# The unread matmuls of the first stage in plain fp32 and in smaller lots, with new order tables

## The chip, the cores and the metric

The kernel runs on one core of a Trainium2 chip. The metric is the device time of one execution in microseconds, the median over several runs. A separate execution was taken by the hardware profiler; all spans, waits and durations below come from it. TensorE (PE) multiplies, VectorE (DVE) and ScalarE (ACT) do the elementwise work, GpSimd (POOL) clears and copies a few tiles at the start, and SyncE (SP) issues the DMAs.

## The reference

```
kv  = einsum('bhsd,bhse->bhde', k, v)             # 8 batches, 8 heads, 576 rows, 64 columns
out = einsum('bhsd,bhde->bhse', q, kv)
att = out / sqrt(mean(out*out, -1) + 1e-6) * g_norm
x   = att with the heads joined                   # 8 x 576 x 512
u   = x + ((x^T @ U) @ V)^T                       # rank 32, over the sequence
res = u + relu(u @ w_ch1) @ w_ch2                 # 512 -> 2048 -> 512
```

## The kernel before, in words

Two heads make a pair, four pairs make a batch, and the 4608 rows of the output are worked off in nine blocks of 512 columns (index `j`). Blocks 0 to 2 go through a plain two-layer product in 16 steps `f`: `ffn1` (12 matmuls of 512 columns, from the rows' high and low parts `uth`, `utl` and the weight tile `ws`f into the PSUM tile `h`), then `relu` on ACT and DVE into `hhl`, then `ffn2` (12 matmuls into four tiles `y`). Blocks 3 to 8 go two at a time through a product with seven forms of the weights instead of eight. Every fp32 value that a matmul reads at speed is split into a high and a low fp32r part, which costs ACT and DVE work.

The weights come as 64-bit numbers. For each `f` a DMA brings `raw`f; ACT copies its top bits (`dec0<-raw`), DVE shifts the rest into place (`dec1<-raw`), ACT makes the high part (`ws<-dec`) and DVE the low part.

Everything ahead of the first full `ffn1` is the first stage (`first_stage`). There each pair p of batch 0 passes through: `kv` (ten matmuls of 64 columns into `pp`), `kvc` (ACT copies into `kvb`), `out` (four matmuls into `y` and one into `pp`), `sq` (ACT squares into `x`), `red` (DVE sums), `root` (ACT), `rms` (DVE, four short instructions), `mul` (DVE, writes the normed `x`), `turn` (four matmuls against the unit matrix, back into `y`), `t` (five matmuls against `U`), `t4` (casts into `st`), `mix` (adds the rank-32 part to `y`), `uh` and `ul` (high and low part of the block's rows), and a `tail` of 64 columns. Tiles of pair 0 to 3 are `y_174` to `y_177`; the normed rows are `x_90` for pair 0 and `x123` for the others. The weights of `f` = 0 (`w1raw`, `w2raw`) are decoded here too, and step `f` = 0 of `ffn1` into `pp_172` is part of this stage. The first instruction of the main loop on PE is `ffn1` of `f` = 1, the first row `h<-uth,ws`.

No scheduler orders the instructions. Every step has a number in a table: `PAIR0`, `ONCE` and `RAWS` for the first stage and the raw loads, `DECODE`, `DUOS`, `PREP`, `CPAT`, `REST`, `FORMSAT` and `FOLLOW` for what is threaded between the blocks' matmuls. `at(place, step)` files a step and `do(limit)` calls all filed steps below a limit in ascending order. An engine's program is the order of these calls. Each engine runs its own in order and waits on semaphores for the others.

Some matmuls write to a PSUM tile that nothing reads (`spare`, called `h_109` in the rows of the order). The first eight (`WARM`) multiply the cleared tile `kvb[0]` in fp32, ahead of everything else. The others are the steps `x0` to `x7` of `ONCE`: each calls `fill()`, eight matmuls of the cleared tile `t4s[1]` with itself in fp32r. A matmul of plain fp32 appears in the trace as two passes, one of fp32r as one.

From batch 1 on, two pairs are worked off together by `run_step` (matmuls into `ph` and `pt`, after which the next `kv_sb` tile is read), then `sq`, `red`, `rms`, `mul` on `x_90`, then `t_both` (`pt<-x,u`). `kv_sb` has one buffer, so its next load waits until `run_step` has read the last.

Of the kernel before, what the change touches and what calls it, by code (L numbers as in the profile page):

```python
# [10 lines left out]
F32 = mybir.dt.float32  # L11
# [26 lines left out]
REST = {0: 3.7, 1: 51.3, 2: 83.9, 4: 112.05, 6: 169.0}  # L38
RESTLOAD = {1: 39.6, 2: 72.15, 4: 102.5, 6: 162.85}
FORMSAT = {3: ((89.5, 89.96, 90.05, 90.15, 92.95, 93.05, 93.25, 96.15, 96.95, 97.45, 98.95), (91.45, 91.61, 93.35, 94.3, 94.45, 96.3, 96.6, 97.8, 97.85, 98.85, 100.6)), 5: ((144.15, 146.21, 148.3, 148.9, 150.4, 151.4, 151.6, 153.25, 153.85, 154.45, 155.35), (146.55, 146.91, 148.75, 149, 149.45, 150.4, 151.45, 152.15, 152.8, 154.2, 154.55)), 7: ((195.4, 198.66, 199.8, 202.4, 204.35, 205.25, 206.4, 207.55, 208.35, 208.45, 212.25), (200.55, 201.51, 205.9, 205.95, 206.65, 206.75, 207.25, 207.6, 208.45, 209.3, 211.05))}  # L40
FINISH = {0: (37.15, 36.85, 35.7, 37.2), 1: (65.76, 68.34, 67.85, 68.25), 2: (101.5, 101.6, 100.75, 101.6)}
DECODE = ((-16.9, -13.1, -6.25, -3.1), (-3.4, -2.25, 0.35, 1.76), (0.55, 1.97, 2.98, 3.33), (3.34, 3.54, 4.29, 5.84), (5.45, 5.9, 6.45, 6.6), (6.11, 7.96, 8.21, 8.66), (8.47, 8.72, 8.77, 9.72), (10.08, 10.68, 11.63, 12.53), (11.1, 12.64, 13.04, 13.49), (13.05, 13.65, 14.1, 14.4), (14.36, 15.76, 16.21, 17.76), (17.77, 17.92, 20.57, 21.02), (20.13, 21.83, 22.63, 23.03), (22.79, 23.54, 24.14, 24.42), (24.15, 25.45, 27.54, 29.1))
FOLLOWERS = ('relu11_0', 'B11_0', 'relu12_0', 'B21_0', 'less11_0', 't2_0', 'less12_0', 'less21_0', 'relu11_1', 'B11_1', 'relu12_1', 'B21_1', 'less11_1', 't2_1', 'less12_1', 'less21_1', 'T2_0', 'T2_1', 'T1_0', 'T1_1', 'T3_0', 'T3_1', 'B22_0', 'B22_1', 'T4_0', 'T4_1')
FOLLOW = {
# [6 lines left out]
FIRSTKV = 2.95  # L51
GROUPS = ('kvl', 'ql', 'run', 'sq', 'kvc', 'red', 'root', 'rms', 'mula', 'mulb', 't', 'ts', 'turna', 'outa', 'ina', 'turnb', 'outb', 'inb', 't4a', 'mixa', 'adda', 'ga', 't4b', 'mixb', 'addb', 'gb')
DUOS = {
# [14 lines left out]
FORMS = ["A11", "A12", "S2", "S1", "S3", "S4", "A22"]  # L68
WITH = ["B11", "B21", "T2", "T1", "T3", "B22", "T4"]
PREP = ((31.2, 31.35, 33.05, 33.4), (34.4, 36.4, 38.1, 39.45), (36.75, 41.55, 43, 43.7), (42.3, 44.65, 45.3, 46.05), (45.4, 45.65, 46.7, 47.45), (49.95, 50.7, 52.4, 54.45), (52, 53.45, 55.3, 55.55), (55.95, 56.4, 57.25, 57.9), (59.7, 59.8, 61.25, 61.85), (60.1, 62.35, 62.95, 64.15), (63.35, 63.95, 65.35, 65.55), (67.31, 71.35, 71.75, 71.95), (70.95, 72.1, 74.7, 77.05), (75.85, 76.35, 78.15, 80.3), (81.25, 81.95, 84.2, 87.1), (81.95, 87.2, 88.95, 90.65))  # L70
CPAT = [35.8, 31.0, 10.74, 21.85, 14.9, 22.55, 41.95, 23.29, 27.65, 18.45, 27.55, 40.7, 34.95, 31.45, 25.3, 55.7]
WARM = 8
PAIR0 = ((-38.3, -37.9, -35.35, -34.35, -30.7, -30.6, -29.2, -29.1, -22.35, -28.55, -27.15, -23.3, -21.5, -18.45, -13.7, -13.9, -6.45), (-34.6, -33.2, -31.6, -28.95, -28.75, -28.1, -27.3, -25.65, -22.4, -25.15, -23.65, -20.8, -14.4, -12.4, -11.3, -13.99, -7.83), (-29.05, -27.35, -25.5, -24.45, -24.2, -23.45, -22.8, -21.75, -20.75, -21.1, -19.2, -18, -16.6, -11.6, -10.65, 0.56, 0.8), (-28.25, -26.95, -23.4, -23.15, -21.5, -20.85, -19.55, -19.35, -15.15, -18.65, -17.25, -14, -13.5, -11.2, -3.55, -3.47, -2.1))
ONCE = {'uvt': -35.4, 'uvb': -34.1, 'uvu': -31.3, 'vsh': -28.8, 'vsl': -23.5, 'v4': -22.8, 'w1t': -26.5, 'w1b': -25.6, 'w1h': -24.25, 'w1l': -19.25, 'w2t': -23.2, 'w2b': -17.4, 'w2h': -14.4, 'w2l': -4.15, 'f0': -11.85, 'f1': -8.7, 'f2': -7.1, 'x0': -10.85, 'x1': -36.45, 'x2': -31.85, 'x3': -32.4, 'x4': -23.95, 'x5': -40.25, 'x6': -30.55, 'x7': -16.09}
RAWS = (-24.25, -21.45, -11.75, -33.85, 6.9, 3.95, -19.93, 12.43, -17.56, 13.25, 13.81, 10.92)
LOADS = ['kv0', 'q0', 'uv', 'kv1', 'q1', 'kv2', 'q2', 'kv3', 'q3', 'w10', 'w20', 'w11', 'w21', 'w12', 'w22', 'w13', 'w23', 'kv4']
NBLK = B * S // BLK


@with_exitstack  # L80
def build(ctx: ExitStack, tc: tile.TileContext, kv0_in, kv_in, q_in, uv_in, w_in, out):
# [624 lines left out]
    def first_stage():  # L706
# [53 lines left out]
        def fill():  # L760
            for _ in range(8):
                mm(spare[:, 0:P], lhsT=t4s[1], rhs=t4s[1], start=True, stop=True)

        for k in range(8):
            once[f"x{k}"] = fill
# [297 lines left out]
```

## Time and profile before

| | us |
|---|---|
| median of three runs | 827.26 |
| the three runs | 828.61, 827.26, 824.36 |
| the profiled execution | 826.27 |
| its span, first to last instruction | 824.5 |
| PE busy in the span | 818.3 |

The profile's page gives each engine's busy time, its busy share in 40 slices and the granted TensorE clock, the DMA queues, and the chain of work that ended last. The trace behind it answers for stretches: instructions in order of time, the waits and what ended them, and busy times in windows. A matmul's busy time includes its way through the array, so its rate is read from the distance of starts, or from the chain, which counts each stretch once. The column of the granted clock shows 1.00 from the first microsecond on; where the level changes inside the first 15 us is seen only in the distances of the matmuls.

### The profile page before, as it was taken

The page shows a single profiled execution, that of the slowest core. Times are in us where ns is not written, and L with a number is a line of the kernel's source. Part 1 is how long each engine was busy: PE and PEld are TensorE (multiplying, and loading weights), DVE is VectorE, ACT ScalarE, POOL GpSimd, SP SyncE. Part 2 cuts the span into 40 slices and gives each one's busy share as a digit, 9 for nine tenths or more (in the row PEclk, how much of TensorE's full clock was granted, in tenths as well). Part 3 has the DMA queues.
Part 4 walks back from the last instruction along what each step waited for, and adds up shares of the span by engine and source line. Part 5 has one row for each costly group of instructions (what it writes and reads, how often), then busy time and mean ns, then how long its engine had stood idle before and what let it go on. Part 6 is the DMA issues. An engine that isn't in the chain of part 4 may idle for free.

```text
span 824.5 us, 13843 instructions
## 1 busy us (share of the span) xinstructions
PE 818.3 (99%) x5308; PEld 675.2 (82%) x5308; DVE 565.8 (69%) x840; ACT 355.3 (43%) x603; POOL 7.7 (1%) x38
## 2 busy tenths in 40 slices
PE   9999999999999999999999999999999999999998
PEld 9888788788887888887888888888788888888886
DVE  2867566777877566678855798579537974872485
ACT  3855543234323434444525554453255544331541
POOL 3000000000000000000000000000000000000000
PEclk9999999999999999999999999999999999999999
DMA  9956874957767645598789699786676786666665
GB/s 352 410 200 240 306 271 141 329 194 238 246 238 248 206 143 175 148 358 284 258 252 282 183 301 305 228 285 200 199 209 207 220 278 193 180 201 197 196 203 174
DMA packets 109841, 195.34 MB, mean 237 GB/s; under 512 B 10832, under 2 KB 45904, under 8 KB 107984
## 3 DMA queue, kind: packets, MB, share of 16 engines
q1 hardware_dynamic: 109632, 194.33, 72.5%
q8 instruction: 42, 0.69, 0.3%
q14 instruction: 23, 0.19, 0.1%
q10 hardware_dynamic: 144, 0.13, 0.0%
HBM read 145.14 MB, written 49.28 MB: 236 GB/s over the span
## 4 chain that ended last, share of the span: by engine, by line
PE 91%; DMA 4%; DVE 3%; ACT 1%; issue 0%; SPq 0%; DVEq 0%; ACTq 0%
PE y L132 68%; PE h L132 14%; PE pt L132 3%; PE ph L132 3%; DMA ut<-xt 2%; PE pp L132 2%; DMA raw<-w_in 2%; DVE dec L122 1%; DMA w1s<-dec 1%; DVE st L122 1%; SPq L122 0%; ACT dec L122 0%; DVE hhl L122 0%; DVE ut L122 0%; DVE ss L122 0%
## 5 line engine op out<-in xcount | busy, mean ns | idle before, releaser
L132 PE MATMUL y<-entry,ring 128*128 128x512 f32 x576 | 135.3, 390 | 0.0
L132 PE MATMUL y<-hhl,ws 128*128 128x512 f32 x540 | 131.3, 392 | 0.0
L132 PEld LDWEIGHTS y<-entry,ring 128*128 128x128 f32 x576 | 107.7, 188 | 22.7 <-issue 0.2
L132 PE MATMUL h<-uth,ws 128*128 128x512 f32 x360 | 119.1, 392 | 0.1
L132 PEld LDWEIGHTS y<-hhl,ws 128*128 128x128 f32 x540 | 100.3, 188 | 21.7 <-issue 0.6
L122 ACT ACTIVATE hhl<-h 128x512 fp32r<-128x512 f32 (+1 forms) x53 | 34.5, 651 | 121.6 <-PE h L132 109.1
L132 PE MATMUL y<-uB,ringw 128*128 128x512 f32 x354 | 84.7, 390 | 0.0
L122 DVE TENSOR_TENSOR h<-y,h 128x512 f32<-128x512 f32 x71 | 48.5, 688 | 51.9 <-PE y L132 43.3
L132 PE MATMUL y<-uT,ring 128*128 128x512 f32 x348 | 83.2, 391 | 0.0
L132 PEld LDWEIGHTS h<-uth,ws 128*128 128x128 f32 x360 | 67.5, 188 | 15.2 <-DVE hhl L122 1.1
L122 DVE TENSOR_TENSOR entry<-h,entry 128x1024 fp32r<-128x1024 f32 x48 | 58.0, 1219 | 31.6 <-ACT entry L122 29.5
L132 PEld LDWEIGHTS y<-uB,ringw 128*128 128x128 f32 x354 | 66.3, 188 | 13.7
L132 PEld LDWEIGHTS y<-uT,ring 128*128 128x128 f32 x348 | 64.9, 188 | 14.1 <-issue 0.4
L122 DVE SCALAR_TENSOR_TENSOR hhl<-h,hhl 128x512 fp32r<-128x512 f32 (+1 forms) x53 | 39.7, 749 | 49.6 <-ACT hhl L122 49.6
L132 PE MATMUL h<-utl,ws 128*128 128x512 f32 x180 | 70.1, 389 | 0.0
L122 ACT COPY h<-y 128x512 f32<-128x512 f32 x70 | 40.6, 587 | 63.4 <-PE y L132 63.3
L122 ACT CAST entry<-h 128x1024 fp32r<-128x1024 f32 x48 | 49.9, 1051 | 40.3 <-PE y L132 23.4
L132 PE MATMUL y<-entry,ringw 128*128 128x512 f32 x216 | 55.3, 391 | 0.0
L132 PE MATMUL y<-hhl,ringw 128*128 128x512 f32 x216 | 54.9, 389 | 0.0
L132 PE MATMUL y<-uT,ringw 128*128 128x512 f32 x210 | 50.6, 390 | 0.0
L132 PEld LDWEIGHTS y<-hhl,ringw 128*128 128x128 f32 x216 | 40.5, 188 | 8.5
L132 PEld LDWEIGHTS y<-entry,ringw 128*128 128x128 f32 x216 | 40.1, 188 | 8.6 <-issue 0.4
(169 smaller groups left out, 1054.3 us busy)
## 6 DMA issues: line engine op xcount, KB each, us to landing
ring<-wd SPq DMA_DIRECT2D x69, 256.0 KB, 3.4
kv_sb<-kv_in SPq DMA_DIRECT2D x14, 1216.0 KB, 7.7
ringw<-wd SPq DMA_DIRECT2D x66, 256.0 KB, 3.4
raw<-w_in SPq DMA_DIRECT2D x30, 511.8 KB, 11.3
ring<-w1s SPq DMA_DIRECT2D x48, 256.0 KB, 3.8
ringw<-w1s SPq DMA_DIRECT2D x48, 256.0 KB, 3.6
ring<-w2s SPq DMA_DIRECT2D x48, 256.0 KB, 4.0
ringw<-w2s SPq DMA_DIRECT2D x48, 256.0 KB, 4.1
```

What stands on the lines that cost most here:

```text
L122: ins = getattr(self.eng, name)(*args, **kw)
L132: ins = nc.tensor.matmul(*args, **kw)
```

## The change: fill matmuls and all order tables

The step `fill` now makes two matmuls in place of eight, and reads the cleared tile as fp32 (two passes each) and not as fp32r. There are fourteen such steps, `x0` to `x13`, and not eight. `WARM` is as it was. All order tables have new numbers. Every other instruction on every engine is there as often as before.

```diff
@@ first_stage @@
+        blank = t4s[1].bitcast(F32)
+
         def fill():
-            for _ in range(8):
-                mm(spare[:, 0:P], lhsT=t4s[1], rhs=t4s[1], start=True, stop=True)
+            for _ in range(2):
+                mm(spare[:, 0:P], lhsT=blank, rhs=blank, start=True, stop=True)
 
-        for k in range(8):
+        for k in range(14):
             once[f"x{k}"] = fill
@@ one of the tables; the others are renumbered in the same way @@
-RAWS = (-24.25, -21.45, -11.75, -33.85, 6.9, 3.95, -19.93, 12.43, -17.56, 13.25, 13.81, 10.92)
+RAWS = (-26.05, -34.85, -12.05, -24.35, 0.8, 10.4, -15.08, 11.83, -22.16, 14.9, 14.61, 16.57)
```

On PE, at the start of the program. `h_109` is the unread tile, `kvq0` and `kvq1` the data of pairs 0 and 1, `kvb` the copied products. Before:

```order
L132 MATMUL h_109<-kvb_102 128x128 x8
L132 MATMUL h_109<-t4_1_98 128x128 x8
L132 MATMUL pp_178<-kvq0_144 64x64 x10
L132 MATMUL h_109<-t4_1_98 128x128 x8
L132 MATMUL y_174<-kvb_102,kvq0_144 128x128 x4
L132 MATMUL pp_178<-kvb_102,kvq0_144 128x128
L132 MATMUL pp_179<-kvq1_148 64x64 x10
L132 MATMUL h_109<-t4_1_98 128x128 x16
L132 MATMUL y_175<-kvb_102,kvq1_148 128x128 x4
```

and after the change:

```order
L132 MATMUL h_109<-kvb_102 128x128 x8
L132 MATMUL h_109<-t4_1_98 128x128 x4
L132 MATMUL pp_178<-kvq0_144 64x64 x10
L132 MATMUL h_109<-t4_1_98 128x128 x2
L132 MATMUL y_174<-kvb_102,kvq0_144 128x128 x4
L132 MATMUL pp_178<-kvb_102,kvq0_144 128x128
L132 MATMUL h_109<-t4_1_98 128x128 x2
L132 MATMUL pp_179<-kvq1_148 64x64 x10
L132 MATMUL h_109<-t4_1_98 128x128 x2
L132 MATMUL y_175<-kvb_102,kvq1_148 128x128 x4
L132 MATMUL pp_179<-kvb_102,kvq1_148 128x128
L132 MATMUL h_109<-t4_1_98 128x128 x4
```

The work on the pairs stands in the same order; the unread lots between them have shrunk.

On PE, from the normed rows of pairs 1 and 2 on, up to the first part of `ffn1` (`pp_172`), after the change. `wf` is the unit matrix or `U`, `st0` to `st2` the `t4` tiles of pairs 1 to 3:

```order
L132 MATMUL h_109<-t4_1_98 128x128 x2
L132 MATMUL pp_178<-x123_119,wf_103 96x128 x5
L132 MATMUL y_176<-wf_103,x123_119 128x128 x4
L132 MATMUL y_175<-wf_103,x123_119 128x128 x4
L132 MATMUL h_109<-t4_1_98 128x128 x2
L132 MATMUL y_175<-v4_99,st0_134 128x4x64 x2
L132 MATMUL pp_179<-x123_119,wf_103 96x128 x5
L132 MATMUL h_109<-t4_1_98 128x128 x2
L132 MATMUL y_176<-v4_99,st1_135 128x4x64 x2
L132 MATMUL y_177<-wf_103,x123_119 128x128 x4
L132 MATMUL y_177<-v4_99,st2_136 128x4x64 x2
L132 MATMUL h_109<-t4_1_98 128x128 x2
```

Before, there is one unread lot of eight in the stretch that corresponds; now there are four lots of two up to here.

On DVE, around the first `run_step` of batch 1, before (`h_704` is the first-layer product of `f` = 5, `ss_774` the sums of the squares):

```order
L122 SCALAR_TENSOR_TENSOR hhl_717<-h_704,hhl_717 128x512
L122 TENSOR_REDUCE ss_774<-x_90 128x18
L122 SCALAR_TENSOR_TENSOR dec1_784<-raw8_648,dec0_104 128x1024
L122 RECIPROCAL r0_775<-ta_776 128x18
```

and after the change (`h_628` is that of `f` = 4, `h_727` that of `f` = 5):

```order
L122 SCALAR_TENSOR_TENSOR hhl_641<-h_628,hhl_641 128x512
L122 TENSOR_TENSOR ws6_701<-dec1_626,ws6_701 128x4x256
L122 SCALAR_TENSOR_TENSOR dec1_708<-raw7_321,dec0_104 128x1024
L122 TENSOR_TENSOR ws7_710<-dec1_708,ws7_710 128x4x256
L122 TENSOR_REDUCE ss_698<-x_90 128x18
L122 SCALAR_TENSOR_TENSOR hhl_740<-h_727,hhl_740 128x512
L122 SCALAR_TENSOR_TENSOR dec1_743<-raw8_471,dec0_104 128x1024
L122 RECIPROCAL r0_699<-ta_700 128x18
```

The `run_step` follows step 4 now and followed step 5 before, and DVE does three decode instructions and a `relu` between its release and the sums' use. On SP, the loads from `raw6` on, after the change (before, `raw9` stood directly behind `raw6` and ahead of both `ut32` loads):

```order
L122 DMA raw6_420<-w_in 128x2047 x2
L122 DMA raw8_471<-w_in 128x2047 x2
L122 DMA ut32_0_91<-q_in 128x576
L122 DMA ut32_1_92<-q_in 128x576
L122 DMA kv_sb_572<-kv_in 128x2432
L122 DMA kv_sb_746<-kv_in 128x2432
L122 DMA ut32_2_93<-q_in 128x576
L122 DMA ut32_3_94<-q_in 128x576
L122 DMA raw9_754<-w_in 128x2047 x2
```

`raw9` has moved behind two `kv_sb` loads, the second of which waits for `run_step`.

## Rows read from the trace of the kernel before

**Rows 1.** The page: engines, busy us, share of the span, instructions.

```profile
PE 818.3 (99%) x5308; PEld 675.2 (82%) x5308; DVE 565.8 (69%) x840; ACT 355.3 (43%) x603; POOL 7.7 (1%) x38
```

**Rows 2.** Waits of PE: us in total, times, longest.

```profile
PE h L132 <- DVE eps L122: 1.1, 1, 1.1
PE ph L132 <- DVE ut L122: 1.0, 2, 0.8
PE ph L132 <- ACT kvb L122: 0.4, 1, 0.4
```

**Rows 3.** PE in order of time: start, busy us, engine, what [idle before].

```profile
1.05 3.78 PE L132 MATMUL h<-kvb 128*128 128x128 f32 x16 [1.05 <-DVE eps L122]
4.49 1.95 PE L132 MATMUL h<-t 128*128 128x128 f32 x8
6.37 1.34 PE L132 MATMUL pp<-kvq 128*64 128x64 f32 x20
...
38.60 0.48 PE L132 MATMUL h<-uth,ws 128*128 128x512 f32 x1
```

**Rows 4.** The chain of waits, first 60 us: start, net us, what.

```profile
9.60 1.81 PE y L132 x8
...
13.11 2.34 PE h L132 x16
...
23.47 0.94 PE y L132 x8
...
27.01 1.09 PE pp L132 x10
...
31.16 1.19 PE y L132 x10
32.35 1.18 PE pp L132 x6
...
45.84 2.72 PE h L132 x12
```

**Rows 5.** ACT and DVE in the first stage, in order of time.

```profile
11.95 0.26 ACT L122 ACTIVATE x<-pp 64x128 f32<-64x128 f32 x1
12.31 0.82 DVE L122 TENSOR_REDUCE wf<-x 128x10 f32<-128x640 f32 x1 [2.71 <-ACT x L122]
...
14.01 0.22 DVE L122 RECIPROCAL wf<-wf 128x10 f32<-128x10 f32 x1 [0.89 <-ACT wf L122]
...
15.55 0.27 DVE L122 TENSOR_TENSOR x<-pp,wf 64x128 f32<-64x128 f32 x1
...
19.48 0.43 ACT L122 COPY kvb<-pp 64x64 f32<-64x64 f32 x2 [1.05 <-PE pp L132]
...
20.95 0.77 ACT L122 CAST dec<-w1raw 128x512 f16<-128x512 bf16 x1
21.74 0.60 ACT L122 ACTIVATE x<-y 128x512 f32<-128x512 f32 x1
...
25.23 1.28 ACT L122 CAST v<-uvs 32x144 fp32r<-32x144 f32 x4
```

**Rows 6.** Loads of the pairs' data (`kvq`), from issue to landing.

```profile
DMA to landing us min/median/max: 3.9/6.5/8.6
```

**Rows 7.** Behind the first `run_step` of batch 1, in order of time.

```profile
67.44 3.02 PE L132 MATMUL y<-hhl,ws 128*128 128x512 f32 x12
67.92 1.35 DVE L122 TENSOR_REDUCE ss<-x 128x18 f32<-128x1152 f32 x1 [1.39 <-ACT x L122]
...
74.45 0.68 DVE L122 TENSOR_TENSOR x<-ph,r 128x512 f32<-128x512 f32 x1
...
78.55 0.85 PE L132 MATMUL pt<-x,u 128*32 128x128 f32 x20
...
84.28 1.36 ACT L122 CAST dec<-raw 128x1024 f16<-128x1024 bf16 x1 [1.47 <-DMA raw<-w_in]
```

**Rows 8.** The chain of waits in the same stretch.

```profile
71.37 12.83 DMA raw<-w_in
```

More of the change, by code (lines that the diff above doesn't have):

```diff
@@ L37 @@
 NEARLY = 1
-REST = {0: 3.7, 1: 51.3, 2: 83.9, 4: 112.05, 6: 169.0}
-RESTLOAD = {1: 39.6, 2: 72.15, 4: 102.5, 6: 162.85}
-FORMSAT = {3: ((89.5, 89.96, 90.05, 90.15, 92.95, 93.05, 93.25, 96.15, 96.95, 97.45, 98.95), (91.45, 91.61, 93.35, 94.3, 94.45, 96.3, 96.6, 97.8, 97.85, 98.85, 100.6)), 5: ((144.15, 146.21, 148.3, 148.9, 150.4, 151.4, 151.6, 153.25, 153.85, 154.45, 155.35), (146.55, 146.91, 148.75, 149, 149.45, 150.4, 151.45, 152.15, 152.8, 154.2, 154.55)), 7: ((195.4, 198.66, 199.8, 202.4, 204.35, 205.25, 206.4, 207.55, 208.35, 208.45, 212.25), (200.55, 201.51, 205.9, 205.95, 206.65, 206.75, 207.25, 207.6, 208.45, 209.3, 211.05))}
@@ L41 @@
-FINISH = {0: (37.15, 36.85, 35.7, 37.2), 1: (65.76, 68.34, 67.85, 68.25), 2: (101.5, 101.6, 100.75, 101.6)}
-DECODE = ((-16.9, -13.1, -6.25, -3.1), (-3.4, -2.25, 0.35, 1.76), (0.55, 1.97, 2.98, 3.33), (3.34, 3.54, 4.29, 5.84), (5.45, 5.9, 6.45, 6.6), (6.11, 7.96, 8.21, 8.66), (8.47, 8.72, 8.77, 9.72), (10.08, 10.68, 11.63, 12.53), (11.1, 12.64, 13.04, 13.49), (13.05, 13.65, 14.1, 14.4), (14.36, 15.76, 16.21, 17.76), (17.77, 17.92, 20.57, 21.02), (20.13, 21.83, 22.63, 23.03), (22.79, 23.54, 24.14, 24.42), (24.15, 25.45, 27.54, 29.1))
+REST = {0: 2.6, 1: 55.85, 2: 88.95, 4: 122.1, 6: 170.25}
@@ new lines @@
+RESTLOAD = {1: 39.45, 2: 80.7, 4: 101.75, 6: 165.75}
+FORMSAT = {3: ((90.35, 90.36, 90.9, 92, 93.25, 93.75, 93.95, 97.05, 97.5, 98.15, 100.1), (90.75, 91.16, 93.8, 94.15, 94.9, 95.45, 95.85, 97.25, 97.75, 99.35, 100.05)), 5: ((142.05, 142.21, 143.8, 147.75, 148.15, 148.25, 149.7, 151.85, 153.2, 153.4, 154.4), (148.55, 149.31, 149.5, 151.35, 151.9, 152, 153.05, 153.75, 153.9, 155.65, 156)), 7: ((199, 199.31, 201.8, 202.45, 203.45, 205.85, 206.5, 209.8, 209.95, 210.6, 211.1), (202.85, 203.96, 206.7, 206.75, 206.85, 207.65, 209.35, 209.9, 211, 211.75, 211.95))}
@@ new lines @@
+FINISH = {0: (34.6, 37.05, 33.15, 34.4), 1: (65.36, 67.59, 68.25, 68.25), 2: (99, 99.2, 99.9, 98.55)}
+DECODE = ((-12.8, -10.05, -5.75, -1.25), (-5.55, -0.15, 0.85, 1.21), (2, 2.32, 3.03, 3.18), (3.19, 4.74, 5.29, 5.49), (5.05, 6.05, 7.3, 7.5), (7.31, 7.91, 8.16, 8.21), (8.52, 8.57, 8.77, 9.17), (9.33, 10.13, 10.88, 11.63), (11.7, 12.14, 12.94, 13.29), (12.3, 13.5, 17.1, 17.45), (13.66, 17.96, 18.41, 19.21), (19.32, 19.72, 20.37, 21.02), (21.03, 21.83, 22.18, 22.48), (22.19, 23.24, 23.29, 23.82), (23.25, 25.85, 27.79, 28.35))
@@ L50 @@
 SB_AT = {3: 96, 5: 152, 7: 208}
-FIRSTKV = 2.95
+FIRSTKV = 3.55
 GROUPS = ('kvl', 'ql', 'run', 'sq', 'kvc', 'red', 'root', 'rms', 'mula', 'mulb', 't', 'ts', 'turna', 'outa', 'ina', 'turnb', 'outb', 'inb', 't4a', 'mixa', 'adda', 'ga', 't4b', 'mixb', 'addb', 'gb')
 DUOS = {
[7 rows of a table removed]
[7 rows of a table added]
 }
@@ L69 @@
 WITH = ["B11", "B21", "T2", "T1", "T3", "B22", "T4"]
-PREP = ((31.2, 31.35, 33.05, 33.4), (34.4, 36.4, 38.1, 39.45), (36.75, 41.55, 43, 43.7), (42.3, 44.65, 45.3, 46.05), (45.4, 45.65, 46.7, 47.45), (49.95, 50.7, 52.4, 54.45), (52, 53.45, 55.3, 55.55), (55.95, 56.4, 57.25, 57.9), (59.7, 59.8, 61.25, 61.85), (60.1, 62.35, 62.95, 64.15), (63.35, 63.95, 65.35, 65.55), (67.31, 71.35, 71.75, 71.95), (70.95, 72.1, 74.7, 77.05), (75.85, 76.35, 78.15, 80.3), (81.25, 81.95, 84.2, 87.1), (81.95, 87.2, 88.95, 90.65))
@@ L71 @@
-CPAT = [35.8, 31.0, 10.74, 21.85, 14.9, 22.55, 41.95, 23.29, 27.65, 18.45, 27.55, 40.7, 34.95, 31.45, 25.3, 55.7]
+PREP = ((31.3, 31.45, 31.95, 34.75), (32, 36.9, 38.2, 39.5), (39.7, 40.85, 41.8, 42.65), (42.6, 42.9, 43.3, 43.65), (45.95, 47.55, 47.65, 48.4), (47.8, 48.65, 49.15, 50.75), (50.75, 53.2, 53.8, 55.7), (53, 54.3, 56.05, 56.25), (58.55, 59.1, 59.95, 60.9), (59.65, 60.3, 62.25, 62.9), (64.05, 64.3, 65.7, 67.35), (66.21, 71.35, 72.45, 72.85), (70.4, 72.2, 74.25, 75.35), (75.7, 76.65, 77.1, 78.25), (77.45, 79.4, 80.2, 90.3), (80.25, 87.85, 91.5, 92.25))
@@ L72 @@
+CPAT = [33.05, 30.9, 13.19, 22.65, 11.8, 18.7, 42.4, 13.29, 36.9, 14.65, 26.05, 37.15, 30.6, 25.35, 27.05, 59.85]
 WARM = 8
-PAIR0 = ((-38.3, -37.9, -35.35, -34.35, -30.7, -30.6, -29.2, -29.1, -22.35, -28.55, -27.15, -23.3, -21.5, -18.45, -13.7, -13.9, -6.45), (-34.6, -33.2, -31.6, -28.95, -28.75, -28.1, -27.3, -25.65, -22.4, -25.15, -23.65, -20.8, -14.4, -12.4, -11.3, -13.99, -7.83), (-29.05, -27.35, -25.5, -24.45, -24.2, -23.45, -22.8, -21.75, -20.75, -21.1, -19.2, -18, -16.6, -11.6, -10.65, 0.56, 0.8), (-28.25, -26.95, -23.4, -23.15, -21.5, -20.85, -19.55, -19.35, -15.15, -18.65, -17.25, -14, -13.5, -11.2, -3.55, -3.47, -2.1))
@@ L74 @@
-ONCE = {'uvt': -35.4, 'uvb': -34.1, 'uvu': -31.3, 'vsh': -28.8, 'vsl': -23.5, 'v4': -22.8, 'w1t': -26.5, 'w1b': -25.6, 'w1h': -24.25, 'w1l': -19.25, 'w2t': -23.2, 'w2b': -17.4, 'w2h': -14.4, 'w2l': -4.15, 'f0': -11.85, 'f1': -8.7, 'f2': -7.1, 'x0': -10.85, 'x1': -36.45, 'x2': -31.85, 'x3': -32.4, 'x4': -23.95, 'x5': -40.25, 'x6': -30.55, 'x7': -16.09}
-RAWS = (-24.25, -21.45, -11.75, -33.85, 6.9, 3.95, -19.93, 12.43, -17.56, 13.25, 13.81, 10.92)
+PAIR0 = ((-39.7, -39.55, -37.25, -33.95, -32.65, -31.4, -31.1, -30.7, -23.45, -30.15, -28.2, -25.35, -22.75, -21.6, -18.95, -22.1, -6.2), (-36.15, -32.95, -32.85, -30.4, -28.65, -28.35, -27.55, -25.35, -19.15, -21.65, -20.3, -16.55, -15.75, -14.1, -12.55, -10.74, -10.53), (-29.55, -27.15, -25.1, -24.3, -23.8, -23.35, -21.9, -20.45, -19.8, -20, -19.9, -18.05, -13.75, -12, -9.95, -3.99, 0.45), (-28.6, -26.8, -24.15, -24.05, -23.15, -21.45, -20.25, -20, -11.75, -15.65, -14.55, -13.25, -11.7, -7.95, -3, -2.72, -2.15))
@@ new lines @@
+ONCE = {'uvt': -36.7, 'uvb': -34.8, 'uvu': -33.25, 'vsh': -32.85, 'vsl': -27.75, 'v4': -25.1, 'w1t': -24.9, 'w1b': -24, 'w1h': -18.65, 'w1l': -15.75, 'w2t': -17.85, 'w2b': -16.05, 'w2h': -14.8, 'w2l': -0.35, 'f0': -9.7, 'f1': -9.15, 'f2': -6.95, 'x0': -37.2, 'x1': -40.3, 'x2': -40.45, 'x3': -31.85, 'x4': -30.6, 'x5': -33.7, 'x6': -37.4, 'x7': -20.55, 'x8': -28.6, 'x9': -21.75, 'x10': -11.55, 'x11': -14.7, 'x12': -8.6, 'x13': -16.9}
+RAWS = (-26.05, -34.85, -12.05, -24.35, 0.8, 10.4, -15.08, 11.83, -22.16, 14.9, 14.61, 16.57)
```

20 rows, old and new, of tables (DUOS, FOLLOW) are left out of this document.

## The prediction

> **What bounds the kernel now.** I read the page's engine line first, then the waits of PE, then PE's first 40 us in order of time and in the chain of waits, and last what ACT, DVE and SP do there. PE is busy 818.3 of 824.5 us and the other engines at most 69% [rows 1]. PE's waits in the whole span come to 2.5 us, of which 1.1 is the start and 1.4 lie in three places by `run_step` and `mix` [rows 2]. So the time is the sum of PE's passes, and a change counts by the passes that it takes away, by the level of the clock that they meet, and by the waits that it opens. Around the span there are 826.27 - 824.5 = 1.8 us, which I leave as they are, and so the end behind the last matmul, whose instructions stand in the same order.
>
> The reader is to see three things in the first stage. The main loop's first matmul starts at 38.60 [rows 3], and from 1.05 on PE goes from one instruction to the next without a recorded wait [rows 2, 3]. Up to 13 us a small pass takes about twice what it takes later: the 16 plain passes from 1.05 to 4.49 are 0.215 us apart [rows 3] and eight `y` passes take 1.81, against 0.94 for eight at 23.47 [rows 4]. That is the low level, 1.2 GHz, against the high one, 2.4 GHz. The level rises inside the double lot at 13.11: sixteen fp32r passes take 2.34 there, where eight took 1.95 at 4.49 [rows 3, 4]; with 0.24 low and 0.105 high (estimates from these two rows) five of them are low, so it rises near 14.2. And the low stretch lasts 13 us although PE does not pause.
>
> **The change, part by part.** Passes first. Before, the eight lots are 64 passes of fp32r; now 28 plain matmuls are 56 passes. A plain pass costs 0.215 low and 0.94 / 8 = 0.12 high, so a lot of two matmuls costs 0.86 or 0.47. No other instruction is added or removed.
>
> Now PE's stream along the new order, with the rise where it is today (case B). 24 unread passes of 0.215 bring it to 6.2, `kv` of pair 0 (1.34 [rows 3]) to 7.5, a lot to 8.4, `out` of pair 0 (1.81 [rows 4], two more passes 0.43) to 10.6, a lot to 11.5, `kv` of pair 1 to 12.8, a lot to 13.7, `out` of pair 1 across the rise to 15.1, four matmuls of fill (0.94) to 16.0, `t` of pair 0 (1.09 [rows 4]) to 17.1, and `kv` of pairs 2 and 3 (half of 1.34 each, an estimate) to 18.5. The data has landed by then: the last load of a pair's data is issued ahead of 5 us and takes 8.6 at most [rows 6].
>
> From there ACT and DVE decide. In the new order ACT does the copies of `kvb` (0.43), the four `v4` casts (1.28), the top bits of `w1raw` (0.77) and the squares of both pairs 2 and 3 (2 x (0.60 + 0.26)) [rows 5]: 4.2 us, to 22.7. DVE sums pair 3 (0.82) and then takes pair 2 from the reciprocal to the last write of `x`, 14.01 to 15.82, or 1.8 [rows 5]: 25.3. PE reaches that point at about 25.2, so its lots just fill the time. What PE still has to do before the main loop is, from the second fence of the order on: two `t` (2 x 1.09), three `turn` with `mix` (3 x 1.19), three tails (1.18 for two, so 1.8), the four parts of the first `ffn1` (2.72 for twelve such passes) [rows 4] and four lots (1.9): 12.1 us. The decodes of `f` = 0 and 1 hide behind this work; ACT and DVE do the same number of them before and now. The main loop starts at 25.3 + 12.1 = 37.4, not 38.6: **1.2 us gained**.
>
> Case A: the level rises earlier. The trace of before has no early rise, so its bounds are: not before 4.4, since the first sixteen plain passes run low to their end [rows 3], and upward anything. Between these I take 7.0, near the end of the first 24 passes, which are now one unbroken run of plain fp32. The reason is in the low stretch itself: before, plain passes and fp32r passes alternate there (16 plain, 8 fp32r, `kv` plain, 8 fp32r, `out` and `kv` plain, then the rise), and the one thing that the change does to this stretch is to make all of it plain. Then `kv` of pair 0 ends at 7.3, a lot at 7.8, `out` at 9.0, a lot at 9.5, `kv` of pair 1 at 10.2 (landed), a lot at 10.6, `out` at 11.8, the four matmuls at 12.8. Pair 0's `x` came 4.4 us behind the end of its main `out` passes (11.41 to 15.82 [rows 4, 5]); these now end at 8.8, so `t` of pair 0 waits to 13.2 and ends at 14.3; `kv` of pairs 2 and 3 end at 15.7; 4.2 + 0.8 + 1.8 as above give `x` of pair 2 at 22.5, and 12.1 more 34.6: **4.0 us gained**.
>
> The Trainium skill speaks against case A: "TensorE: Matmul & The Clock Gate", Part 1, says that the warm-up is a budget of time and not a number of matmuls, so that whatever is issued first runs low. By that rule the kind of the unread matmuls is without effect and case B holds. The row agrees so far that the rise came on a timetable of its own, not at the sixteenth or the twenty-fourth pass; no run shows whether plain passes move it.
>
> Behind the first stage all tables are renumbered, and PE's three waits there (1.4 us) may move or go. One place comes out late. The first `run_step` of batch 1 now follows `f` = 4 and its `t` still comes four half-steps of 2.72 [rows 4] later, 10.9 us. Before, DVE could sum the squares 0.5 us after `run_step` (67.44 to 67.92), the last write of `x` ended at 75.13 and PE came at 78.55 [rows 7], 3.4 us to spare. Now DVE has the low part of `ws6`, the shift of `raw7` and the low part of `ws7` ahead of the sums (about 1.2 each, an estimate by the 1.35 of the sums), and the second needs ACT's top bits of `raw7` (1.36 [rows 7]) behind the squares. That puts the sums some 5.5 us behind `run_step` and the end of `x` about 11.6, so PE waits **0.7 us**, between nothing and 2.
>
> Sum of case A: 826.27 - 4.0 + 0.7 = 823.0. It is 3.3 below the profiled execution and 4.3 below the median of 827.26; that median and its neighbours lie 4.2 us apart, so a single execution tells less than this.
>
> **The rivals.** *The level rises at the same place* (case B). For it: both kinds of pass come at the same distance in the low stretch, 0.215 and 1.95 / 8 = 0.24 [rows 3], so they may well load the engine alike, and 3.4 us of plain passes did not raise it. Against it: something in 4.5 to 13 us held the level down, and the fp32r lots are what goes. Time 826.27 - 1.2 + 0.7 = 825.8.
>
> *The level rises later, and the kernel is slower than before.* All the unread operands are cleared tiles. If it is the work on real data that raises the level, the thinner lots and the order, with `t` of pair 0 waiting on DVE, could bring the rise later. If it comes only behind `kv` of pair 3, the stretch from 13.7 to 18.5 runs low: ten passes of `out` 2.15, eight unread 1.72, ten of `t` 2.15 and two `kv` 2.68, together 8.7 and not 4.8 us, and ACT's list hangs on its end. Time 825.8 + 3.9 = 829.7. It decides from about 0.5 us of work moved to the low level, a rise later than 15. Against it: PE's stream has as much plain work before 13 us as before, and more.
>
> *A weight load moved behind a wait stalls ACT.* `raw9` is now issued behind a `kv_sb` load that `run_step` must release. In case A `run_step` ends at 34.6 + (67.44 - 38.60) - 5.44 = 58.0 [rows 3, 7], so `raw9` goes out near 59. ACT takes its top bits ahead of the `relu` of `f` = 6. The load of the same size in that stretch needed 12.83 us [rows 8]; then ACT is free of it at 59 + 12.8 + 1.4 = 73.2, and the `relu` (0.60 and 0.68 for such tiles [rows 5, 7]) is done at 74.5, where PE wants it at 58.0 + 10.9 + 1.5 + 2.7 = 73.1. Price 1.4, time 824.4. Against it: fewer bytes stand ahead of `raw9` now than stood ahead of that load.
>
> **How the numbers follow.** Case A 0.48, B 0.25, later rise 0.12, `raw9` 0.10, and 0.05 for other waits among the renumbered tables. Forecast: 823.0, of case A. Its own range is 821 to 825, for a rise between 4.4 and 10. The range over all is 820.8 to 829.7. About 0.5% is what a measurement of this kernel can tell from no change: 4.1 us, or 823.1 and 831.4. Case A lies on the lower line and gives about half its chance to faster, 0.25, with 0.07 from the other cases going well: faster 0.32. Slower needs more than the later rise as priced: 0.09. The rest, 0.59, is within.
>
> **What would show it.** In the profile after: the distance of the plain passes and of `kv` (20 passes in 1.34 or 0.7) gives the place of the rise; the first `h<-uth,ws` stands at 34.6 in case A, 37.4 in B, 41 with a later rise. PE's waits should name `pt` of the first `t` after `run_step` with up to 1 us and nothing above. The prediction is wrong if the rise is where it was or later, if the main loop starts later than 36, or if new waits of PE sum to over 3 us.

## The result and the profile after

The changed kernel takes 830.13 us in the median of 7 runs (828.49 to 832.0); the kernel before takes 825.49 (822.66 to 828.61) in the same comparison. The ratio is 1.0054 with an interval of 1.0031 to 1.0077: **slower by about half a per cent**, and just above the forecast range. The profiled execution took 828.49 us, with a span of 826.7.

The page's engine line answers to [rows 1]: busy us, share of the span, instructions.

```profile
PE 814.2 (98%) x5300; PEld 670.4 (81%) x5300; DVE 564.4 (68%) x840; ACT 354.5 (43%) x603; POOL 7.7 (1%) x38
```

PE is busy 4.1 us less than before, and yet the span is 2.2 longer: 6.3 us have become idle time of PE. Where it went is in PE's waits, which answer to [rows 2] (us in total, times, longest).

```profile
PE ph L132 <- DVE x L122: 2.4, 1, 2.4
PE ph L132 <- DVE ut L122: 1.8, 1, 1.8
PE h L132 <- DVE eps L122: 1.1, 1, 1.1
PE ph L132 <- issue: 1.0, 1, 1.0
PE pp L132 <- DVE x L122: 0.9, 2, 0.5
PE pt L132 <- DVE x L122: 0.6, 2, 0.4
PE pt L132 <- DMA kv_sb<-kv_in: 0.6, 1, 0.6
PE y L132 <- DMA ringw<-wd: 0.2, 1, 0.2
```

The start (1.1) is as it was, and `pp <- DVE x` (0.9) belongs to the first stage. The other six are behind it and sum to 6.6 us, against 1.4 in [rows 2]: **5.2 us of new waits behind the first stage** between these two executions. Now PE in order of time, which answers to [rows 3].

```profile
1.05 3.70 PE L132 MATMUL h<-kvb 128*128 128x128 f32 x16 [1.05 <-DVE eps L122]
4.58 1.06 PE L132 MATMUL h<-t 128*128 128x128 f32 x8
5.57 0.80 PE L132 MATMUL pp<-kvq 128*64 128x64 f32 x20
...
12.96 1.30 PE L132 MATMUL pp<-x,wf 128*96 128x128 f32 x10 [0.53 <-DVE x L122]
...
34.90 0.40 PE L132 MATMUL h<-uth,ws 128*128 128x512 f32 x1
...
275.62 0.50 PE L132 MATMUL ph<-v,t 128*128 128x288 f32 x2 [2.35 <-DVE x L122]
...
380.77 0.53 PE L132 MATMUL ph<-v,t 128*128 128x288 f32 x2 [1.75 <-DVE ut L122]
```

Eight unread passes from 4.58 take 1.06 where they took 1.95, and twenty `kv` passes 0.80 and not 1.34: the level is high from about 4.5 us. The main loop starts at 34.90 against 38.60, 3.7 us earlier. The span is 2.2 longer, so the rest of the kernel takes 5.9 us more. The two long waits of 2.35 and 1.75 us are the last rows here.

The longest, in full: ACT and DVE ahead of 275.62, the `mix` of the last pair of batch 3, which needs `ph` free of `run_step(4,0)`.

```profile
268.08 1.05 ACT L122 CAST wf<-dec 128x1024 fp32r<-128x1024 f32 x1 [2.41 <-DMA w2s<-wf]
269.03 1.08 ACT L122 ACTIVATE x<-ph 128x512 f32<-128x512 f32 x2
...
270.31 1.35 DVE L122 TENSOR_REDUCE ss<-x 128x18 f32<-128x1152 f32 x1 [3.92 <-ACT x L122]
...
274.79 0.68 DVE L122 TENSOR_TENSOR x<-ph,r 128x512 f32<-128x512 f32 x1
```

The squares of `run_step(4,0)` were due when its matmuls had ended, but ahead of them in ACT's order stands the cast of the twelfth weight sum (counted from 0) into `wf`. That tile has one buffer, and the store of the eleventh sum had to leave it first. The chain of waits (start, net us, what) has that store, the same thing some 100 us earlier (ahead of the cast of the third sum), and the `kv` load in between.

```profile
160.51 9.93 DMA w2s<-wf
...
226.22 8.56 DMA kv_sb<-kv_in
...
262.84 5.16 DMA w2s<-wf
```

In the kernel before the cast stands behind the squares (ACT in order of time):

```profile
269.47 1.09 ACT L122 ACTIVATE x<-ph 128x512 f32<-128x512 f32 x2 [0.47 <-PE ph L132]
...
272.90 1.03 ACT L122 CAST wf<-dec 128x1024 fp32r<-128x1024 f32 x1
```

The table `PREP` says it: a sum has four places (adds, sums, cast, low part with both stores). The eleventh sum's store and the twelfth's cast stood at 71.95 and 74.7, and the squares at 74.3; now they are at 72.85, 74.25 and 74.95.

### The profile page after: what moved, and what is told of

Its sections match the earlier page's. It is cut to its first block, busy times and chain, and to the rows that moved or that the text cites. A ratio compares the mean times of both kernels' runs of the same rounds, so it can differ in the third digit from the quotient of the medians.

```text
span 826.7 us, 13835 instructions
## 1 busy us (share of the span) xinstructions
PE 814.2 (98%) x5300; PEld 670.4 (81%) x5300; DVE 564.4 (68%) x840; ACT 354.5 (43%) x603; POOL 7.7 (1%) x38
## 4 chain that ended last, share of the span: by engine, by line
PE 83%; DMA 5%; DVE 5%; ACT 3%; issue 2%; SPq 1%; DVEq 0%; ACTq 0%
PE y L132 65%; PE h L132 11%; PE pt L132 3%; PE ph L132 3%; DMA w2s<-wf 2%; PE pp L132 1%; DVE dec L122 1%; DMA kv_sb<-kv_in 1%; SPq L122 1%; DMA ringw<-w1d 1%; DMA ut<-xt 1%; DVE x L122 1%; ACT dec L122 1%; DMA ringw<-wd 1%; DVE ws L122 1%
## 5 line engine op out<-in xcount | busy, mean ns | idle before, releaser
L132 PEld LDWEIGHTS y<-uB,ringw 128*128 128x128 f32 x354 | 66.2, 188 | 13.9 <-issue 0.2
```

The source lines that it names most:

```text
L132: ins = nc.tensor.matmul(*args, **kw)
```

## The experiments

**Which half of the change costs.** First, the new first stage alone: the fill, `PAIR0`, `ONCE`, the decodes of `f` = 1 and 2 and the raw loads of the first stage from the changed kernel, and every later table from the kernel before. Two of these tables, against the changed kernel:

```diff
-FIRSTKV = 3.55
+FIRSTKV = 2.95
...
-PREP = ((31.3, 31.45, 31.95, 34.75), ...
+PREP = ((31.2, 31.35, 33.05, 33.4), ...
```

> The changed first stage (fill, PAIR0, ONCE, the decodes of f=1 and 2, the raw loads of that stage) with all later tables of the kernel before. Theory T1 (the loss comes from the new tables behind the first stage, whatever the start): main loop at 34.9 us as after the change, PE waits behind it about 1.4 us as before, time 3.7 us below the kernel before: 821.8 where that takes 825.5. Theory T2 (the rest cannot follow an earlier start, its loads and the ACT and DVE work keep their own pace): main loop at 34.9, but PE waits behind it grow by about 3.7 us, time 825.5.

Measured: 824.38 us, ratio 1.0004 (0.9988 to 1.0021). No gain, no loss. The first theory has the waits right, but its gain of 3.7 us is not there, although the main loop of the profiled execution starts at 35.52. The waits behind the first stage are back near those of [rows 2].

```profile
PE ph L132 <- DVE ut L122: 0.8, 1, 0.8
PE ph L132 <- ACT kvb L122: 0.5, 1, 0.5
PE h L132 <- DVE hhl L122: 0.2, 1, 0.2
```

Then the reverse, the old first stage with the new later tables (`FIRSTKV = 3.55` and so on in the kernel before).

> The first stage of before (fp32r lots of eight, its order) with the new later tables. T1: main loop at 38.6, PE waits behind it near the 6.9 us of idle that the changed kernel shows, time about 3.7 us above the changed kernel: 833.8. T2: with the late start the waits shrink by as much, time 826 to 830.

Measured: 831.89 us, ratio 1.0083 (1.0054 to 1.0113). The later tables cost 0.8%, some 7 us, with the old start too, and PE waits 6.5 us behind the first stage, as the first theory has it. The wait of `ph` is there, in PE's waits:

```profile
PE ph L132 <- DVE x L122: 2.2, 1, 2.2
```

Behind it the clock is at the low level for a stretch. The row gives the stretch, its length, the busy us and instructions of PE, PEld, DVE, ACT and POOL, the granted clock, the DMA share and GB/s.

```profile
279.70:283.20 3.50, 3.50 (x10) 2.73 (x10) 3.40 (x8) 0.00 (x0) 0.00 (x0) 0.51 0.47 146
```

**The kind of the unread passes.** The kernel before with the same 64 passes as plain fp32, eight lots of four:

```diff
+        blank = t4s[1].bitcast(F32)
...
-            for _ in range(8):
-                mm(spare[:, 0:P], lhsT=t4s[1], rhs=t4s[1], start=True, stop=True)
+            for _ in range(4):
+                mm(spare[:, 0:P], lhsT=blank, rhs=blank, start=True, stop=True)
```

> The kernel before with its eight lots as four plain fp32 matmuls each, so the same 64 passes in the same places. If plain passes raise the clock's level and fp32r ones do not: the rise comes between 4.5 and 8 us, the main loop starts between 35 and 37 us, time 822 to 824. If the kind of pass is without effect (order, or the moment of the start, decides): rise near 14, main loop at 38.6, time 825.5.

Measured: 823.47 us, ratio 0.9983 (0.9964 to 1.0002), which the runs do not tell from no change. In the profiled execution the level is high from 5.2 us and the main loop starts at 34.79.

And the changed kernel with its 56 passes as fp32r, fourteen lots of four:

```diff
-            for _ in range(2):
-                mm(spare[:, 0:P], lhsT=blank, rhs=blank, start=True, stop=True)
+            for _ in range(4):
+                mm(spare[:, 0:P], lhsT=t4s[1], rhs=t4s[1], start=True, stop=True)
```

> The changed kernel with each lot of two plain matmuls as four fp32r ones, so the same 56 passes in the same places. If the kind of pass decides: the rise comes at 14 us or later, the main loop starts at 37.4 or later, time 2.5 us or more above the changed kernel, 832.6. If not: rise near 4.5, main loop at 34.9, 830.1.

Measured: 830.98 us, ratio 1.008 (1.0053 to 1.0108): slow like the changed kernel, with overlapping intervals. In its trace the level rises early as well, without a plain lot behind the first sixteen.

```profile
4.49 1.14 PE L132 MATMUL h<-t 128*128 128x128 f32 x8
5.55 0.80 PE L132 MATMUL pp<-kvq 128*64 128x64 f32 x20
```

Up to here it issues what the kernel before issues, where these rows read 1.95 and 1.34 [rows 3]. So the same instructions go with a rise at 4.6 us in one execution and at 13.9 in another (by the granted clock), and an early rise needs no plain lot. Whether plain lots make it likelier, one profile each does not show.

**Whose tables.** Putting back one group of tables at a time: the weight sums and their copies (`PREP`, `CPAT`) of before in the changed kernel, the `run_step` pipeline (`DUOS`, `FIRSTKV`, `REST`, `RESTLOAD`) of before in the changed kernel, and the changed `PREP` and `CPAT` in the kernel before. One line of the first edit:

```diff
-CPAT = [33.05, 30.9, 13.19, ...
+CPAT = [35.8, 31.0, 10.74, ...
```

> The changed kernel with PREP and CPAT (the sums of the weights, their stores, the copies of the weights) of the kernel before. Theory P (the new places of the weight sums make ACT wait for a store of its own buffer, the pairs' squares come late and PE waits): the wait of 2.4 us at 273 and those near 176 go, time 3 to 5 us below the changed kernel, 825 to 827. Theory D (the places of the pairs' work, DUOS, make the waits): waits stay, time 830.

> The changed kernel with DUOS, FIRSTKV, REST and RESTLOAD (the pairs' work and the rows kept between blocks) of the kernel before. Theory P: the wait near 273 stays, time about 829 to 831. Theory D: the waits of ph and pt go, time 824 to 826. If both tables count, or only fit each other, time between or above.

> The kernel before with PREP and CPAT of the changed kernel. Theory P: waits of 2 us and more of PE appear in the blocks 1 and 2, time 3 to 5 us above the kernel before, 827 to 829. Theory D: time as before, 824.

Measured: 837.4 us, ratio 1.0151 (1.0116 to 1.0186); 850.76, ratio 1.033 (1.0286 to 1.0373); 834.43, ratio 1.0118 (1.0083 to 1.0152). All are worse than either kernel, the first and the third by more than any case put down for them. So blame can't be laid on a table: the groups are timed against each other. The third shows how. It puts the new `PREP` beside the old `DUOS`, and its chain of waits has the same store ahead of the same cast and squares.

```profile
267.88 4.44 DMA w2s<-wf
...
272.39 1.05 ACT wf L122
273.44 1.16 ACT x L122 x3
```

The same trace gives what the prediction had lacked: the first stage of the kernel before, unchanged, with an early rise.

```profile
4.41 1.09 PE L132 MATMUL h<-t 128*128 128x128 f32 x8
5.43 0.80 PE L132 MATMUL pp<-kvq 128*64 128x64 f32 x20
...
34.27 0.48 PE L132 MATMUL h<-uth,ws 128*128 128x512 f32 x1
```

With the rise near 4.4 in both, the old stage reaches the main loop at 34.27 and the new one at 34.90.

**Are the lots needed.** The kernel before without its eight lots (the eight plain matmuls at the start stay; what is left out is read by nobody):

```diff
-            for _ in range(8):
-                mm(spare[:, 0:P], lhsT=t4s[1], rhs=t4s[1], start=True, stop=True)
+            pass
```

> The kernel before without its eight unread lots (the first eight unread matmuls stay). If the unread lots only fill time in which PE would wait for ACT and DVE: the main loop starts where ACT and DVE hand over, 33 to 35 us when the clock rises early, time 821 to 823. If they hold the clock up: PE pauses, the level rises late or falls again in the first 35 us, the main loop starts at 40 or later, time 826 or more.

Measured: 819.69 us, ratio 0.9941 (0.9921 to 0.9962), **faster than both kernels**. PE, in order of time:

```profile
4.76 1.23 PE L132 MATMUL pp<-kvq 128*64 128x64 f32 x20
6.52 1.16 PE L132 MATMUL y<-kvb,kvq 128*128 128x128 f32 x8 [0.53 <-ACT kvb L122]
...
9.45 1.13 PE L132 MATMUL y<-kvb,kvq 128*128 128x128 f32 x8 [0.64 <-ACT kvb L122]
...
31.48 0.48 PE L132 MATMUL h<-uth,ws 128*128 128x512 f32 x1
```

The level rises inside the first `kv` and stays high through the pauses; the main loop starts at 31.48, earlier than either case had it. That is 2.8 us ahead of the early start of the same stage with its lots (34.27); the rest of the 4.8 us between the medians has no row of its own.

**Four places.** The local theory names four orders in the changed kernel: the twelfth cast (above), the third cast, which waits for the 9.93 us store ahead of the squares of `run_step(2,1)`, the `kv` load for batch 4 (issued at 226.22, wanted at 234), and the stores of `xt` of pair 1 of batch 5, issued on SP ahead of the load of `ut32` that PE's wait at 380.77 hangs on. That load leaves SP here:

```profile
373.41 0.45 SPq L122 DMA_DIRECT2D ut<-xt  x1
```

It takes 6.5 us to landing, to 379.9, and DVE's sum starts at 379.96; that the sum waits for it is worked out from these times, since the profile puts the wait down to PE. First the one cast alone (of a table's long lines only the entry that changes is shown):

```diff
-(70.4, 72.2, 74.25, 75.35)
+(70.4, 72.2, 75.2, 75.35)
```

> The changed kernel with one number different: the cast of the twelfth weight sum at 75.2 and not 74.25, behind the squares of run_step(4,0) on ACT and not ahead of them. Theory L: ACT no longer waits for the store of the eleventh sum ahead of the squares, the 2.74 us pause of PE near 273 goes to under 0.5 and the time is 827.7 (2.4 less than the 830.1 of the changed kernel). Rival S: the squares were late for another reason, the pause stays above 2 us, 830.

Measured: 826.35 us, ratio 1.0026 (1.0002 to 1.0049); between the two ratios lie 0.28%, 2.3 us, though their intervals overlap. The order on ACT, in order of time, is as meant.

```profile
267.86 1.09 ACT L122 ACTIVATE x<-ph 128x512 f32<-128x512 f32 x2 [0.47 <-PE ph L132]
...
271.29 1.04 ACT L122 CAST wf<-dec 128x1024 fp32r<-128x1024 f32 x1
```

On PE the same `mix` bears no wait now, where it bore 2.35 us:

```profile
275.13 0.50 PE L132 MATMUL ph<-v,t 128*128 128x288 f32 x2
```

Other waits vary between executions: the one at 379 is 0.38 us here, with nothing moved there, and 1.16 us are new at 448. So what each place is worth by itself is shown for this cast alone.

Then all four:

```diff
-(42.6, 42.9, 43.3, 43.65)
+(42.6, 42.9, 45.3, 45.45)
-    4: ((62.05, 70.9,
+    4: ((60.05, 70.9,
-105.3, 106.5, 110.65
+105.3, 107.2, 110.65
```

> The changed kernel with four places of its later tables put back in relation to their neighbours: the cast of the twelfth weight sum behind the squares of run_step(4,0) (74.25 to 75.2), the cast of the third sum behind the squares of run_step(2,1) (43.3 to 45.3, its low part 43.65 to 45.45), the load of kv for batch 4 two half-steps earlier (62.05 to 60.05), and the stores of xt of pair 1 of batch 5 behind the load of ut32 for pair 0 (106.5 to 107.2). Theory L (the loss sits in these local orders): the PE pauses at 176, 234, 273 and 379 us (0.8 + 0.5, 0.84, 2.74 and 2.14 between matmul starts, about 0.28 of each being a normal distance) go, 5 us, and the time is 825 (ratio to before 1.000). Rival S (the tables fit each other only as a whole, and a wait taken away comes back behind it): two or more of the pauses come back elsewhere, 828 to 831.

Measured: 827.08 us, ratio 1.0023 (1.0004 to 1.0041), a miss for the local theory as put. The four pauses are gone, and a new one stands at 226.8: the `kv` load now leaves SP ahead of the `ut32` loads, and DVE's sum waits for one of those.

```profile
219.91 0.37 SPq L122 DMA_DIRECT2D kv_sb<-kv_in  x1
220.38 1.41 SPq L122 DMA_DIRECT2D ut<-xt  x2
...
228.28 0.76 DVE L122 TENSOR_TENSOR ut<-ph,ut 128x576 f32<-128x576 f32 x1 [2.53 <-DMA ut<-xt]
...
229.10 0.85 PE L132 MATMUL ph<-v,t 128*128 128x288 f32 x2 [1.95 <-DVE ut L122]
```

The granted clock behind it is low again for one stretch (columns as above).

```profile
229.10:232.60 3.50, 3.50 (x9) 2.94 (x10) 1.50 (x3) 1.04 (x1) 0.00 (x0) 0.51 0.91 325
```

So the `kv` load was put behind the four loads of `ut32`, the other three places as above:

```diff
-    4: ((62.05, 70.9,
+    4: ((60.7, 70.9,
```

> As the kernel with four places moved, but the load of kv for batch 4 goes out behind the four loads of ut32 (place 60.7) and no longer ahead of them (60.05). Theory L (the loss is these local orders): the pause that the first try opened at 226.8 us (2.34, and 3.4 us of clock at 0.5 behind it) goes and none of the four comes back, 827.1 - 2.1 - 1.7 = 823.3, ratio to before 0.999. Rival S (a place moved always costs elsewhere): a pause of over 1 us somewhere in 200 to 240 us, 826 to 828.

Measured: 823.88 us (822.23 to 825.65), ratio 1.0000 (0.9986 to 1.0015), where 823.3 was expected. Four places among more than seven hundred take back the whole loss. Of its waits behind the first stage two are left.

```profile
PE ph L132 <- ACT hhl L122: 1.7, 1, 1.7
...
PE ph L132 <- DMA ut<-q_in: 0.3, 1, 0.3
```

The longer one stands at 170.05, ahead of `run_step(2,1)`, where the changed kernel waited 1.0 us; it is none of the four, and why it grew stays open.

**Without lots in the new order.** Two kernels: the one with four places (in its first form, with the `kv` load ahead), and the new first stage with the later tables of before, each with the fourteen lots left out (`pass` in `fill`).

> As the kernel with four places moved, without the fourteen unread lots (the eight plain matmuls at the start stay). If the lots only take time on PE, the main loop starts near 31.5 as in the kernel before without its lots, and the time is 825 - 3.4 = 821.6. If the lots hold the clock up or cover pauses, the rise of the level moves behind 10 us or the main loop starts at 34 or later: 825 or more.

> The new order of the first stage without its fourteen lots, and all later tables as before. If the new order is worth something once no lots stand in it, the main loop starts ahead of the 31.48 us that the kernel before has without lots, and the time is under its 819.7. If the two orders are worth the same: 819.7 within 1, main loop at 31 to 32. If the new order needs the lots (t of pair 0 waits for DVE, pauses bring the level down): 821 to 824.

Measured: 829.07 us, ratio 1.004 (1.002 to 1.006), and 822.23, ratio 0.9971 (0.9949 to 0.9994). In the second the main loop starts at 34.13 and not at 31.48, since the new order waits more where the lots stood:

```profile
12.80 1.30 PE L132 MATMUL pp<-x,wf 128*96 128x128 f32 x10 [1.43 <-DVE x L122]
...
22.59 1.33 PE L132 MATMUL pp<-x,wf 128*96 128x128 f32 x10 [1.27 <-DVE x L122]
...
34.13 0.39 PE L132 MATMUL h<-uth,ws 128*128 128x512 f32 x1
```

Even so it comes no later than with its lots (34.90 and 35.52); the old order only gains more by losing them. The first of the two is 2 us slower than its partner with lots, although its main loop starts at 33.94 and not at 36.07. Its waits behind the first stage sum to 5.6 us and not 2.8; the one near 227 is longer (2.6 for 1.95), and that pause too is followed by the low level. Why they grow stays open.

**Both kernels once more,** for what differs between executions.

> The kernel before, unchanged, profiled once more. If its operations fix the moment of the rise: 13.9 us again, first h<-uth of the main loop at 38.6. If the moment differs between executions: a rise at 4 to 7 us and the main loop at 34.5 to 35.5, as it was with plain lots.

> The changed kernel, unchanged, profiled once more. If the pauses are of its order: the same places (176, 234, 273, 379 us) with the same 0.8, 0.8, 2.7 and 2.1 us within 0.5. If they are chance of the transfers, at other places or sizes.

Measured: the kernel before took 828.5 us, with the late rise again, and with a long wait that its first profile does not have.

```profile
38.53 0.48 PE L132 MATMUL h<-uth,ws 128*128 128x512 f32 x1
...
165.55 0.50 PE L132 MATMUL ph<-v,t 128*128 128x288 f32 x2 [2.62 <-DVE ut L122]
```

The changed kernel took 828.68, with three of the four pauses in their places: 0.88 us between matmul starts at 176 (0.81 in the first profile), 2.38 at 272 (2.74) and 2.00 at 379 (2.14). The one at 234 is not there; its wait was 0.57. Behind the first stage PE waits 3.5 us in this profile of the kernel before and 5.5 in that of the changed one, so the 5.2 us of the first pair of profiles is 2.0 in the second: one pair is a sample here too.

## Why the prediction was wrong, point by point

**Two terms of the sum failed.** In the runs the forecast of -4.0 + 0.7 us stands against +4.5 (ratio 1.0054). The -4.0 of the first stage measured nothing (the new first stage alone: 1.0004), and the 0.7 us (between 0 and 2) for all tables behind it measured 4.1 us (1.0054 less 1.0004), about 7 with the old first stage (1.0083), and 5.2 in PE's waits of the first two profiles.

**The 0.7 was one place taken for all.** The prediction's own bound for being wrong, over 3 us of new waits, is passed. The prediction priced one place, the first `run_step` of batch 1, from a window of the trace, and took it for the whole; the case "other waits among the renumbered tables" got 0.05. That one place was priced fairly: the sums start at 63.43, 5.2 us behind the end of `run_step` (5.5 was worked out), and PE's `t` at 69.33 bears no wait. The four places that cost were never looked at. Two of them show in the numbers: a cast moves ahead of the squares while the stretch from the store of the single buffer to its next write shrinks. For the twelfth cast it goes from 2.75 half-steps (74.7 - 71.95) to 1.4 (74.25 - 72.85), 3.8 us at 2.72 each, under the 5.16 us that the store took; for the third from 1.6 (45.3 - 43.7) to 0.65 (43.3 - 42.65), 1.8 us, under 9.93.

**In the profile the first stage came out as case A has it, by luck.** Taken: rise at 7.0, main loop at 34.6, `t` of pair 0 waiting 0.4. Measured: 4.5, 34.90, 0.53. But the reason given, an unbroken run of plain passes, falls: with fp32r lots the changed kernel rises at 4.6, and the unchanged first stage of before rises at 4.3 in one execution. Against that execution the new stage is 0.6 us later, not 4.0 earlier, and the new first stage alone measured 1.0004. The 38.60 from which the gain was counted is one way in which the kernel before runs: seen at 13.9 and 13.8 us (profiled executions of 826.27 and 828.5, high among its own runs) and at 13.5 with the new later tables. The prediction said that a single execution tells less than the runs, but still took its low stretch for a property of the code. One reading in it is off, with little effect: 0.24 us is the busy time of eight fp32r passes divided by eight, while their starts are 0.213 apart at the low level, the same as of plain passes, and 0.111 at the high one.

The Trainium skill, "TensorE: Matmul & The Clock Gate", Part 1, was used against case A and half read: the same section says that the number of slow matmuls differs from run to run of one kernel. The traces agree, with 13.9 and 4.3 us for one first stage; but the spread here is far wider than the 6, 11 or 14 slow matmuls that the Trainium skill gives there for one kernel: 86 slow passes in one execution and 15 in the other. By that rule the 38.60 of one execution was no base to count a gain from.

**The rivals.** Case B and the later rise did not come. `raw9` was issued at 59.66 (59 was worked out) and ACT took its top bits at 69.37, and no wait of PE follows from it. The slower outcome came by the side that had been given almost nothing.

**Taken together:** 826.27 - 3.7 + 5.2 gives 827.8; the profiled execution took 828.49.

## What to carry to other kernels

Where a change renumbers a whole schedule, list for every tile with one buffer the distance from its release to its next write, before and after, and compare it with the duration of the transfer between them; then ask who stands behind the waiting instruction on its engine. One sampled place is no price for seven hundred. And a start-up stretch read from one execution is a sample: look at a second execution before a saving is counted from it.

## What the runs showed of the hardware

The moment of the rise scatters and depends on more than the code up to it. The record of the granted clock begins in each trace with the rise, which is why the column shows 1.00 ahead of it; at that moment the starts of the matmuls go from 0.213 to 0.111 us apart. It came at 13.9, 13.8, 13.5 and 4.3 us with the first stage of before, and between 4.2 and 7.3 us in the thirteen other profiles: plain lots, fp32r lots in the new order, or none. Whether the old fp32r lots make the late rise likelier, or it is chance, stays open. Three of four against none of thirteen speaks against pure chance, but the runs without a profile don't show the moment, and the early one of the four ran on another chip than the two late ones whose chips are on record. The 823.47 of plain lots in the old order, whose ten runs end at 824.64 where those of before reach 828.41, speaks for the first.

The clock falls to 1.2 GHz behind some pauses in the main loop and not behind others as long. In the seventeen profiles there are twelve such falls ahead of the program's end, in or just behind waits of PE of 1.9 to 4.5 us (among them the 2.2, 1.95 and 2.6 us told above); none comes at a wait under 1.8. Six waits of 2.0 to 2.6 us have no fall behind them, among them the 2.35 of the changed kernel's first profile and the 2.62 of the second profile of the kernel before. In the second profile of the changed kernel, the pause at 272 is followed by such a stretch (columns as above):

```profile
275.10:278.60 3.50, 3.50 (x11) 2.73 (x10) 3.40 (x8) 0.00 (x0) 0.00 (x0) 0.51 0.46 144
```

Eleven of the twelve stretches last 3.4 us, one 6.8 (behind a wait of 4.4). At half the clock a stretch of 3.4 us costs about 1.7 on top of the pause before it; that is an estimate from the granted clock, which no run measures by itself.
